# Uncut last weighted sums, both gate products behind the next filling product, and two low pieces moved to GpSimd

## The chip, the cores and the metric

The kernel runs on one core of a Trainium2 chip. The metric is the device time of one execution in microseconds (us); the median of several runs is compared. Five engines matter: TensorE (PE for matmuls, PEld for its weight loads), VectorE (DVE), ScalarE (ACT), GpSimd (POOL) and SyncE (SP, which here issues DMAs and reads expert numbers).

## What is computed

The reference is an attention in which a query sees only the keys of its own hash bucket, followed by a mixture of experts that gives each token to one expert.

```python
mask = q_bucket[:, :, :, None] == k_bucket[:, :, None, :]
scores = np.where(mask, scale * q @ k.T, -1e9)
attn = exp(scores - max) / (sum + 1e-9)
x = (attn @ v) as 3072 tokens x 512
logits = x @ w_gate;  e_idx = argmax(logits)
gate_w = softmax(logits)[e_idx];  eom = sigmoid(x @ w_output_gate)
out[token] = gate_w * eom[e_idx] * (relu(x @ w1[e]) @ w2[e])
```

There are 4 batches of 8 heads, 768 positions of 64 numbers; 8 experts with w1 of 512x1024 and w2 of 1024x512. Everything is float32.

## The kernel before, in words

**Products in three parts.** A float32 product of good precision is made of three products of rounded operands: each operand is split into a high part (rounded to the format fp32r) and a low part (operand minus high part), and high x high, high x low and low x high are summed (`product`, line 386). Making a low part is one subtraction with both inputs in the on-chip memory.

**Two phases.** Attention works through 16 pairs of heads in steps; at its end stands the switch to the experts. The 3072 tokens are routed batch by batch; the last batch's routing can only be finished when the last head pair is summed. To fill TensorE meanwhile, 256 tokens of the fullest expert, known from the first three batches, are gathered early, and the eight filling products `fill(0)` to `fill(7)` (w1 of that expert, 12 matmuls each, `up` line 386; ReLU on ScalarE, line 396; the low part on VectorE, line 397, called by `low()`) are laid between the steps of the last routing. All this is an order written out by hand: within that block each engine executes its instructions in the order of the program text, so an instruction that waits holds up those behind it on its engine.

**The place of the change** is this block. In order of the text it holds:

- `fill(0)`;
- the four pieces of the first w2, of 128x1024 numbers: the high parts (`w2_round`, lines 218 and 220) of pieces 2 and 3 on ScalarE, then the low parts (`w2_low`, line 225) of all four on VectorE. Before the third low part stand the three `late_low` subtractions (line 1124), halves of w1's low part, 128x512 each, on VectorE;
- the last weighted sums (`weighted`, line 764): six chunks of two matmuls each, accumulated in `ps_a`; after the sixth, VectorE copies the sum to the second half of the tile `ot` (line 767). After the first chunk's matmuls VectorE's transposition `rows` (line 787) of the first half of `ot` and its four DMAs on SP (line 794) stand in the order;
- `add_pair(hf, ...)`: three matmuls of 128 tokens each (line 831) that add the last head pair's share to the gate logits of half `hf` of the batch, and VectorE's addition (line 832). `add_pair(1)` reads the second half of `ot`;
- from there the routing's chain: `best`, `choose`, the transposition of the second half, `prefix`, `gates`, `ranks`, `cols`, `hot`, `table` (line 294), `entries`, with fills and lows between; then the second product of the early tokens (`down_rows`), the gathers, and the experts in order of their size.

The tiles of the four pieces rotate through five buffers named `w2l`: four hold the raw pieces, the first low part goes into the fifth, and the low part of piece i goes into the buffer of raw piece i-1.

Of the kernel before, what the change touches and what calls it, by code (L numbers as in the profile page):

```python
# [10 lines left out]
F32 = mybir.dt.float32  # L11
# [5 lines left out]
ALU = mybir.AluOpType  # L17
# [6 lines left out]
P = 128  # L24
# [35 lines left out]
def f32(ap):  # L60
    return ap.bitcast(F32)
# [3 lines left out]
def lsh_attention_then_moe(  # L65
# [10 lines left out]
    nc = tc.nc  # L76
# [17 lines left out]
    def signs():  # L94

        t = gp.tile([P, P], F32, name="t_ob")
        nc.scalar.dma_start(t, proj[:, D + 3:])
        return t
# [121 lines left out]
            e.tensor_scalar(hi, p[0], 1.0, 0.0, ALU.mult, ALU.add)  # L220
        return hi

    def w2_low(pool, p, hi):
        lo = pool.tile([P, 2, DM], F32R, name="w2l", bufs=NFB // 2 + 1)
        nc.vector.tensor_tensor(lo, p[0], f32(hi), ALU.subtract)
        return [(hi[:, j], lo[:, j]) for j in range(2)]

    def compared(e, out, x, y, op):
# [75 lines left out]
    ps_t = ctx.enter_context(tc.tile_pool(name="ps_t", bufs=2, space=PSUM))  # L304
    ps_a = ctx.enter_context(tc.tile_pool(name="ps_a", bufs=1, space=PSUM))
    ps_m = ctx.enter_context(tc.tile_pool(name="ps_m", bufs=1, space=PSUM))
# [204 lines left out]
    with ExitStack() as actx:  # L511
# [32 lines left out]
        def load(g, heads=(0, 1)):  # L544
            st = pairs[g]
            st.setdefault("qk", [])
            for j in heads:
                t = hp.tile([P, S], F32, name="qk", bufs=4)
                nc.sync.dma_start(t, qkT[2 * g + j])
                st["qk"].append(t)  # L550
# [15 lines left out]
        def project(g, pp=None, heads=(0, 1)):  # L566
            st = pairs[g]
            if pp is None:
                pp = ps_m.tile([P, HS], F32, name="ps_m")
            for j in heads:  # L570
                for m in range(2):
                    r = 32 * (2 * j + m)
                    nc.tensor.matmul(pp[r:r + 32], pjc[:, m], st["qk"][j][:, m * HS:(m + 1) * HS],
                                     start=True, stop=True)
            bt = hp.tile([P, HS], BF16, name="bt", bufs=2)
            rs = slice(D * heads[0], P)
            nc.vector.tensor_scalar(bt[rs], pp[rs], thr[rs], scl[rs], ALU.is_gt, ALU.mult)
            st["bt"] = bt
# [122 lines left out]
        def soft(s, sc, mn):  # L701
            if s % GROUP == 0:
                sums[s // GROUP] = terms[s // GROUP % len(terms)]
            pr = sc.rearrange("p a b -> p (a b)")
            k = s % GROUP
            nc.scalar.activation(pr, pr, AF.Exp, bias=mn, scale=-1.0,  # L706
                                 accum_out=sums[s // GROUP][:, k, 0:1])
            return pr

        def normal(s0):  # L710

            rs = sp.tile([P, GROUP], F32, name="rsum")
            nc.vector.tensor_reduce(rs, sums.pop(s0 // GROUP), AX.X, ALU.add)
            nc.vector.reciprocal(rs, rs)  # L714
            for k in range(GROUP):
                e = nc.vector if s0 + k == NSTEP - PER - GROUP else nc.gpsimd
                e.tensor_scalar(live[s0 + k], live[s0 + k], rs[:, k:k + 1], 0.0, ALU.mult, ALU.add)  # L717
# [79 lines left out]
        def routing(b):  # L797
# [26 lines left out]
                                        pm[:, :, 0:n, 0:2 * E].rearrange("p t i c -> p t c i"), AX.X, ALU.add)  # L824

            def add_pair(hf, i):
                pm = ps_m.tile([P, 3, 32], F32, name="ps_m")
                hs = slice(hf * 3, hf * 3 + 3)
                for t in range(3):
                    qs = slice((hf * 3 + t) * P, (hf * 3 + t + 1) * P)  # L830
                    nc.tensor.matmul(pm[:, t], pairs[b * H // 2 + i]["ot"][:, qs], wgt[:, i], start=True, stop=True)
                nc.vector.tensor_tensor(st["lgt"][:, hs], st["lgt"][:, hs], pm[:, :, 0:2 * E], ALU.add)
# [163 lines left out]
        for b in range(B - 1):  # L996
            r = routing(b)
# [12 lines left out]
        r = routing(B - 1)  # L1010
        s0 = 12 * (NP - 1)
        lp = H // 2 - 1
# [141 lines left out]
        with tc.manual_schedule(engines=MANUAL | {mybir.EngineType.SP}):  # L1154
            t = signs()
            load(0)
            load(1)
            for bb in halves[:2]:
                nc.vector.memset(bb, 0.0)
            for rs in terms:  # L1160
                nc.vector.memset(rs, 1e-9)
            make_identity(nc, ident)
            for bb in halves[2:]:
                nc.gpsimd.memset(bb, 0.0)

            idle = ps_t.tile([P, 3, P], F32, name="ps_t")

            def turn_idle(n):
                for i in range(n):
                    nc.tensor.transpose(idle[:, i % 3], ident, ident)  # L1170

            turn_idle(12)
            first_heads(t)
            turn_idle(1)
            live = {}
            raw = []

            def softs(n):
                for _ in range(n):
                    if raw:  # L1180
                        s = raw.pop(0)
                        live[s] = soft(s, *live[s])
                        if s % GROUP == GROUP - 1:
                            ready.append(s - s % GROUP)

            ready = []

            def normals():
                while ready:
                    normal(ready.pop(0))  # L1190

            def now(when):
                for fn in around.get((s, when), ()):
                    fn()

            for s in range(PER):
                live[s] = scores(s)
                raw.append(s)
                if 0 < s < PER - 1:
                    turn_idle(1)  # L1200
                if s > 2 and s % 2:
                    normals()
                softs(1)
                for fn in at.get(s, ()):
                    fn()

            for s in range(PER, NSTEP + LAG, 2):
                k = s % PER
                both = range(s, s + 2)
                for x in both:  # L1210
                    if x < NSTEP:
                        live[x] = scores(x)
                        raw.append(x)
                    if x == PER:
                        project(1)
                    if x == PER + 1:
                        for y in range(2):
                            transposed(y, live.pop(y))
                if k == 0 and s > PER:
                    softs(2)  # L1220
                    now("early")
                    normals()
                    now("amid")
                    softs(2)
                    normals()
                    for when in ("before", "matmuls", "behind"):
                        now(when)
                    softs(1)
                elif k == 4 or s == PER:
                    normals()  # L1230
                for x in both:
                    if s > PER:
                        transposed(x - LAG, live.pop(x - LAG))
                if s < 2 * PER or k == 0:
                    softs(1)
                for x in both:
                    for fn in at.get(x, ()):
                        fn()


            ep, hs = early["ep"], early["h"]
            w2s = []
            lows = []

            def fill(f):
                lows.append(up(early["w1"], early["x"], hs, [f], CAP0))

            def low():
                lows.pop(0)()

            fill(0)
            for i, (p, hi) in enumerate(zip(w2p, early["w2h"] + [w2_round(ep, p, nc.scalar) for p in w2p[2:]])):
                if i == 2:
                    for cc in range(1, NCC):
                        late_low(cc)
                w2s += w2_low(ep, p, hi)
            for c in range(NT):
                weighted(2 * NP - 1, c)
                if c == 0:
                    rows(NP - 1, 0, False)  # L1260
                if c == 2:
                    r["add_pair"](0, lp)
            fill(1)
            low()
            r["add_pair"](1, lp)
            fill(2)
            low()
            r["best"]()
            r["choose"]()
            rows(NP - 1, 1, False)  # L1270
            fill(3)
            low()
            r["prefix"]()
            fill(4)
            r["gates"]()
            low()
            r["ranks"]()
            fill(5)
            low()
            fill(6)  # L1280
            r["cols"]()
            low()
            fill(7)
            r["hot"]()
            r["table"]()
            low()
            r["entries"]()
            gid0 = lead_slots(EARLY)
            low()

    mp = ctx.enter_context(tc.tile_pool(name="mp", bufs=1, reuse_waits="tile"))
    with tc.manual_schedule(engines=MANUAL):
# [18 lines left out]
        for r in range(E):  # L1311
# [3 lines left out]
            if r:  # L1315
                hs = new_h()
                w2s = []
# [93 lines left out]
    with tc.If(nr > 0):  # L1411
# [12 lines left out]
        with tc.For_i(0, nr, 1):  # L1424
# [13 lines left out]
            for r in range(E):  # L1438
                more = nc.values_load(left[0:1, r:r + 1], min_val=0, max_val=NTOK)
                with tc.If(more > 0):  # L1440
                    w1s = [w1_piece(wpool, r, cc) for cc in range(NCC)]
                    w2s = []
# [64 lines left out]
```

## Time and profile before

| what | us |
|---|---|
| median of 3 runs (lowest to highest) | 686.34 (686.2 to 687.45) |
| the profiled execution | 686.96 |
| its span, first to last instruction | 685.1 |
| TensorE busy | 674.8 (98%) |
| VectorE, ScalarE, GpSimd busy | 472.6, 435.2, 407.9 |

The profiled execution took 1.86 us more than its span; that part lies outside all instructions. A time of a part is read in the trace as the distance between starts of instructions, since the durations of matmuls and of neighbours on one engine overlap a little.

### The profile page before, as it was taken

To read this page: it belongs to the slowest core of one execution; us is meant where nothing else is said; L and a number is where in the kernel's file an instruction comes from. 1 tells how busy PE (TensorE), PEld (TensorE's weight loads), DVE (VectorE), ACT (ScalarE), POOL (GpSimd) and SP (SyncE) were. 2 spreads that over 40 slices of the span, in tenths; PEclk is the share of its full clock that TensorE was granted. 3 is DMA by queue.
4 is the path that set the end of the run, shared out by engine and by line. 5 is a ranking of instruction groups with operands and counts; after the bars stand their busy time and mean duration, and the time that the engine had idled before them with its cause. 6 is when DMAs were issued, how large, how long until landed. Compare 5 with 4: busy or idle time off the path is not lost. (4 is left out here: it accounts for less than half of the span.)

```text
span 685.1 us, 17346 instructions
## 1 busy us (share of the span) xinstructions
PE 674.8 (98%) x6549; PEld 537.1 (78%) x6549; DVE 472.6 (69%) x1055; ACT 435.2 (64%) x889; POOL 407.9 (60%) x545
## 2 busy tenths in 40 slices
PE   8999999999999999999999999999999999999996
PEld 4767675767676767676767889889999999989995
DVE  7878887888877888878977834463646565646540
ACT  6898998898889898988998214431515243445041
POOL 6878766577856778656888156344273737374002
PEclk9999999999999999999999999999999999999998
DMA  5544554354543445442535135634667666665332
GB/s 167 162 125 101 132 123 109 78 131 104 130 118 82 111 114 118 107 112 59 144 101 175 24 106 193 207 107 149 222 193 235 210 207 220 216 222 198 124 98 79
DMA packets 96612, 96.14 MB, mean 140 GB/s; under 512 B 57839, under 2 KB 76839, under 8 KB 96520
## 3 DMA queue, kind: packets, MB, share of 16 engines
q1 hardware_dynamic: 79704, 72.88, 38.4%
q0 software_dynamic: 5200, 13.31, 5.7%
q10 hardware_dynamic: 11616, 8.75, 4.5%
q8 instruction: 54, 0.88, 0.6%
q14 instruction: 38, 0.31, 0.1%
HBM read 63.83 MB, written 17.50 MB: 119 GB/s over the span
## 5 line engine op out<-in xcount | busy, mean ns | idle before, releaser
L717 POOL TENSOR_SCALAR sc<-sc,rsum 128x768 f32<-128x768 f32 x191 | 171.5, 914 | 75.7 <-DVE rsum L714 35.4
L698 DVE TENSOR_SCALAR_CACHE_REDUCE sc<-ps_s 128x768 f32<-128x768 f32 x192 | 176.4, 955 | 22.1 <-PE ps_s L695 20.5
L706 ACT ACTIVATE sc<-sc,mn 128x768 f32<-128x768 f32 x192 | 178.9, 952 | 1.5 <-DVE sc L698 1.3
L695 PE MATMUL ps_s<-kh,qhl 64*128 64x384 f32 x768 | 149.1, 401 | 0.6 <-DMA qhl<-qhl 0.5
L764 PE MATMUL ps_a<-pts,vt 128*64 128x384 f32 x768 | 131.2, 490 | 0.0
L396 ACT ACTIVATE hh<-ps_s 128x256 fp32r<-128x256 f32 (+8 forms) x40 | 29.1, 727 | 157.8 <-PE ps_s L386 157.8
L753 ACT COPY pts<-ps_t 128x384 f32<-128x384 f32 x188 | 92.6, 494 | 24.2 <-PE ps_s L746 20.4
L764 PEld LDWEIGHTS ps_a<-pts,vt 128*64 128x64 f32 x768 | 52.3, 137 | 66.8 <-issue 61.5
L746 PEld LDWEIGHTS ps_t<-ident,sc 64*128 64x128 f32 x1140 | 81.9, 139 | 20.2 <-POOL sc L717 10.8
L386 PE MATMUL ps_s<-xh,w1h 128*128 128x256 f32 (+7 forms) x288 | 95.9, 333 | 0.0
L360 POOL DMA_INDIRECT xq<-x_dram,idx x75 | 82.0, 1093 | 23.2 <-issue 19.3
L386 PE MATMUL ps_s<-xlo,w1h 128*128 128x256 f32 (+7 forms) x288 | 95.6, 332 | 0.0
L386 PE MATMUL ps_s<-xh,w1l 128*128 128x256 f32 (+7 forms) x288 | 95.3, 331 | 0.0
L397 DVE SCALAR_TENSOR_TENSOR hl<-ps_s,hh 128x256 fp32r<-128x256 f32 (+8 forms) x40 | 34.0, 849 | 76.8 <-ACT hh L396 76.8
L746 PE MATMUL ps_t<-ident,sc 64*128 64x64 f32 x1140 | 86.8, 223 | 0.0
L695 PEld LDWEIGHTS ps_s<-kh,qhl 64*128 64x128 f32 x768 | 76.6, 187 | 1.7 <-DMA qhl<-qhl 0.8
L695 PE MATMUL ps_s<-kl,qhl 64*128 64x384 f32 x384 | 66.5, 333 | 0.0
L695 PE MATMUL ps_s<-bb 64*128 64x384 bf16 x384 | 65.3, 327 | 0.8 <-DMA bb<-bt 0.3
L372 POOL TENSOR_SCALAR xh<-xt 128x512 fp32r<-128x512 f32 (+5 forms) x21 | 12.0, 569 | 78.8 <-DVE xt L369 78.8
L386 PEld LDWEIGHTS ps_s<-xh,w1h 128*128 128x128 f32 x288 | 54.2, 188 | 1.8 <-issue 0.6
L753 ACT COPY pts<-ps_m 128x384 f32<-128x384 f32 x94 | 45.2, 481 | 15.6 <-PE ps_m L746 12.2
L386 PEld LDWEIGHTS ps_s<-xlo,w1h 128*128 128x128 f32 x288 | 54.1, 188 | 1.3 <-DVE xlo L343 0.2
(272 smaller groups left out, 1398.3 us busy)
## 6 DMA issues: line engine op xcount, KB each, us to landing
w_raw<-in_w_dram SPq DMA_DIRECT2D x31, 512.0 KB
qk<-in_qkT_dram SPq DMA_DIRECT2D x32, 384.0 KB
qhl<-qhl SPq DMA_DIRECT2D x62, 192.0 KB
xh<-in_w_dram SPq DMA_DIRECT2D x14, 512.0 KB
xlo<-in_w_dram SPq DMA_DIRECT2D x14, 512.0 KB
vt<-in_v_dram SPq DMA_DIRECT2D x16, 384.0 KB
x_dram<-xb SPq DMA_DIRECT2D x60, 96.0 KB
yt<-y_dram ACTq DMA_DIRECT2D x14, 256.0 KB
```

The costliest lines, as they stand in the source:

```text
L360: nc.gpsimd.indirect_dma_start(out=xq[:, k * P:(k + 1) * P], out_offset=None, in_=x_dram.rearrange("n (a f) -> (n a) f", a=NB32), in_offse ...
L372: nc.gpsimd.tensor_scalar(xh, w[:, :, 0:n], 1.0, 0.0, ALU.mult, ALU.add)
L386: nc.tensor.matmul(ps, l, r, start=first and k == 0, stop=last and k == len(pairs) - 1)
L396: nc.scalar.activation(hh, ph, AF.Relu)
L397: return lambda: nc.vector.scalar_tensor_tensor(hl, ph, 0.0, f32(hh), ALU.max, ALU.subtract)
L695: nc.tensor.matmul(ss[:, h, 0:HS], q[rs, c:c + P], k[rs, 0:HS], start=(i == 0), stop=(i == 3))
L698: nc.vector.tensor_scalar(sc, ss[:, :, 0:HS], MASKED, None, ALU.min, ALU.min, accum_out=mn)
L706: nc.scalar.activation(pr, pr, AF.Exp, bias=mn, scale=-1.0, accum_out=sums[s // GROUP][:, k, 0:1])
L717: e.tensor_scalar(live[s0 + k], live[s0 + k], rs[:, k:k + 1], 0.0, ALU.mult, ALU.add)
L746: nc.tensor.transpose(trs[h][:, c], pr[r, c * P:(c + 1) * P], ident[r, r])
L753: (nc.vector.tensor_copy if h and s and (last or s % PER == 0 or s in (3, 5)) else nc.scalar.copy)(pts[:, :, t * P + h * hq:t * P + (h + 1 ...
L764: nc.tensor.matmul(st["av"][n * D:(n + 1) * D], st["v"][:, n if g else hf, c], blocks[hb][n][:, c], start=(c == 0), stop=(c == NT - 1))
```

## The change

It does four things. The six chunks of the last weighted sums follow each other without `add_pair(0)` between the third and the fourth. Both `add_pair` calls stand behind `fill(1)`. `add_pair(0)` takes its accumulator from the two buffers `ps_t` instead of the single `ps_m`, for every caller. And the low parts of pieces 2 and 3 of the first w2 are made by GpSimd instead of VectorE; their place in the text, behind the `late_low` subtractions, stays.

```diff
-    def w2_low(pool, p, hi):
+    def w2_low(pool, p, hi, e):
         lo = pool.tile([P, 2, DM], F32R, name="w2l", bufs=NFB // 2 + 1)
-        nc.vector.tensor_tensor(lo, p[0], f32(hi), ALU.subtract)
+        e.tensor_tensor(lo, p[0], f32(hi), ALU.subtract)
         return [(hi[:, j], lo[:, j]) for j in range(2)]
...
             def add_pair(hf, i):
-                pm = ps_m.tile([P, 3, 32], F32, name="ps_m")
+                pool, name = (ps_m, "ps_m") if hf else (ps_t, "ps_t")
+                pm = pool.tile([P, 3, 32], F32, name=name)
...
                 if i == 2:
                     for cc in range(1, NCC):
                         late_low(cc)
-                w2s += w2_low(ep, p, hi)
+                w2s += w2_low(ep, p, hi, nc.vector if i < 2 else nc.gpsimd)
             for c in range(NT):
                 weighted(2 * NP - 1, c)
                 if c == 0:
                     rows(NP - 1, 0, False)
-                if c == 2:
-                    r["add_pair"](0, lp)
             fill(1)
             low()
-            r["add_pair"](1, lp)
+            for hf in range(2):
+                r["add_pair"](hf, lp)
             fill(2)
             low()
             r["best"]()
```

## Rows read from the trace of the kernel before

**Rows 1.** Busy time by stretch (us; PE, PEld, DVE, ACT, POOL; clock, DMA): the last full one

```profile
650.00:670.00 20.00, 20.00 (x111) 18.52 (x110) 8.29 (x8) 9.44 (x12) 1.99 (x2) 1.00 0.30 91
```

**Rows 2.** Timeline of TensorE (start, us, engine, line), switch to the experts

```profile
376.44 2.16 PE L764 MATMUL ps_a<-pts,vt 128*64 128x384 f32 x12
378.52 0.85 PE L831 MATMUL ps_m<-wgt,ot 128*128 128x32 f32 x6
379.31 2.16 PE L764 MATMUL ps_a<-pts,vt 128*64 128x384 f32 x12
381.39 0.39 PE L386 MATMUL ps_s<-xh,w1h 128*128 128x256 f32 x1
...
382.80 0.28 PE L386 MATMUL ps_s<-xh,w1l 128*128 128x256 f32 x1
383.53 0.86 PE L831 MATMUL ps_m<-wgt,ot 128*128 128x32 f32 x6 [0.45 <-DVE ot L767]
384.22 0.37 PE L386 MATMUL ps_s<-xh,w1h 128*128 128x256 f32 x1
```

**Rows 3.** Timeline of TensorE: the sums of an earlier half, uncut

```profile
356.04 4.09 PE L764 MATMUL ps_a<-pts,vt 128*64 128x384 f32 x24
360.06 0.27 PE L746 MATMUL ps_t<-ident,sc 64*128 64x64 f32 x1
```

**Rows 4.** Timeline of VectorE, same stretch

```profile
375.33 2.84 DVE L225 TENSOR_TENSOR w2l<-w2l,w2h 128x1024 fp32r<-128x1024 f32 x2
378.09 1.29 DVE L1124 TENSOR_TENSOR w1l<-w_raw,w1h 128x512 fp32r<-128x512 f32 x2
...
379.89 2.54 DVE L225 TENSOR_TENSOR w2l<-w2l,w2h 128x1024 fp32r<-128x1024 f32 x2
382.35 0.57 DVE L787 STREAM_TRANSPOSE xb<-ot 128x384 f32<-128x384 f32 x1
...
382.93 0.54 DVE L767 COPY ot<-ps_a 128x384 f32<-128x384 f32 x1
```

**Rows 5.** Timelines of ScalarE and GpSimd, same stretch

```profile
376.82 1.98 ACT L218 CAST w2h<-w2l 128x1024 fp32r<-128x1024 f32 x2
...
388.43 0.19 POOL L282 CAST t_gh<-gate 128x6 fp32r<-128x6 f32 x1 [12.64 <-DVE gate L882]
```

**Rows 6.** GpSimd's subtractions of two inputs: a group by shape, one pair in the timeline

```profile
L645 POOL TENSOR_TENSOR kl<-qk,kh 128x384 fp32r<-128x384 f32 x30 | 30.4, 1014 | 0.3
...
363.25 2.53 POOL L1119 TENSOR_TENSOR w1l<-w_raw,w1h 128x512 fp32r<-128x512 f32 x2
```

**Rows 7.** Timelines of VectorE and GpSimd: one two-input instruction, twice

```profile
11.64 0.56 DVE L642 SCALAR_TENSOR_TENSOR qhl<-qk,qhl 128x384 fp32r<-128x384 f32 x1
...
39.07 0.51 POOL L637 TENSOR_SCALAR kh<-qk 128x384 fp32r<-128x384 f32 x1
...
39.14 0.85 DVE L642 SCALAR_TENSOR_TENSOR qhl<-qk,qhl 128x384 fp32r<-128x384 f32 x1 [1.83 <-POOL qhl L636]
```

**Rows 8.** Timelines of GpSimd and VectorE: indirect DMAs beside subtractions

```profile
570.05 0.95 POOL L360 DMA_INDIRECT xq<-x_dram,idx  x1 [0.30 <-issue]
...
572.73 2.32 DVE L190 TENSOR_TENSOR w1l<-w_raw,w1h 128x1024 fp32r<-128x1024 f32 x2
...
572.86 1.88 POOL L360 DMA_INDIRECT xq<-x_dram,idx  x1 [0.30 <-issue]
```

**Rows 9.** Timelines: the end of the routing's chain, and w2's first use

```profile
391.52 1.23 POOL L274 TENSOR_TENSOR t_rhs<-t_rhs,t_gl 128x192 fp32r<-128x192 f32 x1
...
393.13 0.78 PE L294 MATMUL ps_t<-t_rhs,lt 128*128 128x128 f32 x6
393.75 0.45 PE L386 MATMUL ps_s<-w2h,hh 128*128 128x512 f32 x1
```

**Rows 10.** The last matmul (timeline of TensorE) and granted clock behind it (by stretch)

```profile
678.68 0.28 PE L386 MATMUL ps_a<-w2h,hl 128*96 128x256 f32 x1
...
681.00:682.00 1.00, 0.00 (x0) 0.00 (x0) 0.00 (x0) 0.00 (x0) 0.00 (x0) 0.62 0.61 174
```

## The prediction, made before the changed kernel was run

> **What bounds the kernel now.** I read the busy time by stretch first. TensorE is busy without a gap through the expert phase [rows 1], and the table of waits shows there nothing of TensorE that is worth naming. So whatever shifts the start of that dense stretch shifts the end by as much, and nothing later takes it back. The one place where the change can act is the switch to the experts, so the timelines of that stretch were next. TensorE runs there: half of the last sums, `add_pair(0)`, the other half, `fill(1)`, then a gap of 0.45 us before `add_pair(1)`, which waits for VectorE's copy to `ot`, then `fill(2)` at 384.22 [rows 2]. From there on it is dense again up to the table's matmuls at 393.13 [rows 9]. The reader is to see why the copy is late: the sums ended at about 381.3, but VectorE works from 375.33 without a pause through two low pieces, three late lows, two more low pieces and the transposition, and reaches the copy at 382.93 [rows 4]. GpSimd meanwhile idles 12.64 us, to 388.43 [rows 5]. My measure for everything below is the start of `fill(2)`: 384.22 before.
>
> **The sums and the products, part by part.** A half of the sums takes 2.08 us (376.44 to 378.52) and the two together 4.16; uncut, an earlier group of the same 24 matmuls takes 4.02, from 356.04 to 360.06 [rows 2, 3]. So the sums end at 376.44 + 4.02 = 380.46. `fill(1)` takes 1.53 (381.39 to the last of its twelve at 382.80, and that one's distance of 0.12 to a next), so it ends at 381.99. The first gate product costs 0.79 (378.52 to 379.31), the second 0.69 (383.53 to 384.22) [rows 2]. Side by side, and if nothing waits, they end at 381.99 + 0.79 + 0.69 = 383.47. That would be a gain of 384.22 - 383.47 = 0.75 us: 0.14 from the uncut sums and about 0.6 from the gap before the second product. A `ps_t` buffer for `add_pair(0)` I cost at nothing: the last transposition copies have left both long before, and the table's product takes the other of the two ten microseconds later.
>
> **What the second product waits for.** It needs the copy to `ot` by 381.99 + 0.79 = 382.78. If VectorE only lost two low pieces (2.54 us [rows 4]), its late lows would end at about 379.9, the transposition at 380.4, the copy, which then waits for the sums, at about 381.1. That is 1.7 us in hand. So the question is whether the pieces given to GpSimd leave VectorE alone.
>
> **GpSimd's price.** Its subtractions of two inputs take 1.014 us for 384 columns and 2.53 for two of 512, so 1.265 each [rows 6]. By the slope between the two a piece of 1024 costs 1.265 + 512 x 0.00196 = 2.27; by two of 512, 2.53. I take 2.4. The pieces themselves are not urgent: the second product of the early tokens starts at 393.75 [rows 9], and two pieces of 2.4 are done ten microseconds earlier even if they wait. When can they start? Their high parts come from ScalarE at 376.82 to 378.80 [rows 5]. The low part of piece 2 goes into the buffer of raw piece 1, which VectorE's second low piece reads until 378.17 (375.33 + 2.84). So GpSimd asks at about 378.2, just when VectorE has begun the first of its three late lows at 378.09 [rows 4].
>
> **Do they disturb each other?** Both kinds of instruction read two inputs from the on-chip memory. The same VectorE instruction takes 0.56 alone and 0.85 when GpSimd began 0.07 earlier an instruction of 0.51 (39.07 to 39.58): it went on at 39.14 + 0.85 - 0.56 = 39.43, 0.15 before GpSimd's end [rows 7]. Of the 29 executions of this line, 25 take 0.82 to 0.86, each begun inside such an instruction of GpSimd. So a VectorE instruction with two such inputs stands still while GpSimd's runs. Who gets in when both wait is shown in the expert phase: GpSimd's indirect DMA takes 0.95, and 1.88 when it begins at 572.86 inside the first of two back-to-back subtractions; the delay of 0.93 ends at 573.79, at the boundary of the two, not behind the second, which ends at 575.05 [rows 8]. Four more indirect DMAs that fall into such pairs do the same. So the one that waits gets in at the next boundary.
>
> **The sum.** A late low takes 0.60 from start to start ((379.89 - 378.09) / 3 [rows 4]). The first ends at 378.69. GpSimd, waiting since 378.2, gets in and runs to 381.09; VectorE goes on 0.15 before that, at 380.94, and ends its second late low at 381.54. GpSimd's second piece, waiting by then, runs to 383.94. The third late low goes on at 383.79 and ends at 384.39. The transposition takes 0.49 (382.35 to its successor at 382.84), the copy 0.54, TensorE starts 0.06 behind it (383.47 to 383.53 before): 384.39 + 0.49 + 0.54 + 0.06 = 385.48. The second product takes 0.69, and `fill(2)` starts at 386.17, 1.95 us later than before. What is queued behind the copy on VectorE (the low part of `fill(0)`, both additions to the logits, all of the routing's chain) moves along; so do TensorE's `fill(2)` and everything behind it, and SP's eight DMAs of the two halves of rows, which follow their transpositions. Nothing in that stretch has spare time to take it back: the last input of the table is ready at 392.75 (391.52 + 1.23) for matmuls at 393.13 [rows 9]. Against the profiled execution, 686.96 + 1.95 = 688.9; against the median of 686.34, **688.3**. The bounds: 2.27 a piece gives 1.95 - 0.26 = 1.7; 2.53 a piece and no early release (0.15 twice) gives 1.95 + 0.26 + 0.3 = 2.5. So 688.0 to 688.9 for this case.
>
> The Trainium skill ("SBUF — State Buffer", section "Who interferes with whom") says that a VectorE instruction with two on-chip inputs and a GpSimd instruction that reads there exclude each other, the first holding the shared ports for its whole length. The trace agrees but for the 0.15 us. By the page alone, with 2.4 a piece, the sum would be 2.25 and the time 688.6.
>
> **The rivals.**
> - *VectorE keeps its place (chance 0.26).* Each piece of GpSimd's that gets in between late lows costs the copy about 2.25 us; with 1.7 in hand, the first costs little and the second decides. If GpSimd's second piece doesn't get in before the third late low, the copy ends near 383.17 and `fill(2)` starts at 383.92: 0.3 gained, 686.0. If neither gets in, all 0.75 is gained, 685.6; then both pieces run behind the late lows, to about 384.7, beside the transposition and the copy, which read one on-chip input or none. For it: no row shows a GpSimd subtraction of 1024 columns, nor one waiting through back-to-back subtractions (the indirect DMA's read is short). Against it: rows 7 and 8 together. This case ends on the other side: not slower.
> - *The clock falls in the new gap (0.10).* TensorE would wait from 382.78 to 385.48, 2.7 us. At the end of the program the last matmul ends at 678.96 and the mean granted clock of the microsecond from 681.00 is 0.62, so it fell from 1.0 to the half level (1.2 GHz) at about 681.24, 2.3 us behind it [rows 10]. No wait of before is that long within the work, and no row shows how long the half level would last. Below, nothing; above, all from `fill(2)` to the table (8.9 us of work [rows 2, 9]) at half speed, 8.9 more. I take one fill, 1.5 us: 689.8. Against it: work surrounds this gap, and only idle follows the other.
> - *The gain is larger than the gap and the cut (0.04).* All that I can add is what the second product's addition gains on VectorE, 0.1; for over 0.2% a stretch would have to be shortened that the trace shows dense.
> - *It does not move (0.06)*: a hold and a half of GpSimd's, or a smaller piece, which eats up the 0.75 and stops there; 686.3.
>
> **How the numbers follow.** 0.2% of this kernel, 1.4 us, is about what a measurement can tell from no change. The forecast (chance 0.54) and the fallen clock (0.10) lie above it: slower 0.64. The cases of 0 to -0.75 us, 0.26 + 0.06, lie within: same 0.32. Faster 0.04. The time is the likeliest case's, 688.3, with its own 688.0 to 688.9. The range goes below to the full gain, 685.4 with the runs' scatter (686.2 to 687.45 before), and above to 690.0, which takes in the short fall of the clock; the long one, and the larger gain, stay out.
>
> **What would show it.** Right: GpSimd's two `w2_low` pieces of 2.3 to 2.6 us in the timeline at about 378.3 and 381.1, the second and third late lows stretched to over 2 us each, the copy to `ot` ending at about 385.4, a gap of 2.5 to 3 us on TensorE before `add_pair(1)`, and `fill(2)` near 386.2 with everything behind it shifted alike. Uncut sums of 4.0 us show the first part; an `add_pair(0)` that waits for the copy too would add 0.8. Wrong: late lows of 0.68 in a row with GpSimd's first piece behind them, a copy done by 382.7 and no gap; or a granted clock below 1.00 between 385 and 390.

## The result, and the profile after

The changed kernel takes a median of 690.26 us (689.39 to 692.76, 7 runs) against 687.40 us for the kernel before (686.20 to 688.33, 7 runs). The ratio is 1.0051, with a 95% interval of 1.0041 to 1.0060: slower by about half a per cent. The forecast was 688.3 in a range of 685.4 to 690.0, so the direction was right and the time lies just above the range. The profiled execution took 690.1 us, with a span of 688.4 us, 3.3 us more than the span before.

The timeline of TensorE in the switch to the experts, in the kernel after (start, us, engine, line; code behind `w2_low` stands one line lower than before), answers to [rows 2]:

```profile
374.37 0.47 PE L821 MATMUL ps_m<-ident,lt 96*128 96x96 f32 x3
...
376.21 4.09 PE L764 MATMUL ps_a<-pts,vt 128*64 128x384 f32 x24
380.23 0.39 PE L386 MATMUL ps_s<-xh,w1h 128*128 128x256 f32 x1
...
381.77 0.75 PE L832 MATMUL ps_t<-wgt,ot 128*128 128x32 f32 x6
385.05 1.23 PE L832 MATMUL ps_m<-wgt,ot 128*128 128x32 f32 x6 [2.53 <-DVE ot L767]
386.08 0.56 PE L386 MATMUL ps_s<-xh,w1h 128*128 128x256 f32 x1
...
388.79 0.28 PE L386 MATMUL ps_s<-xh,w1h 128*128 128x256 f32 x1
...
396.19 0.78 PE L294 MATMUL ps_t<-t_rhs,lt 128*128 128x128 f32 x6
```

The sums run uncut, the two products stand behind `fill(1)`, and the second waits 2.53 us for the copy to `ot`, where it waited 0.45 before. The reason stands in the timeline of VectorE (after; answers to [rows 4]) and in that of GpSimd (after; answers to [rows 5]):

```profile
375.10 2.83 DVE L225 TENSOR_TENSOR w2l<-w2l,w2h 128x1024 fp32r<-128x1024 f32 x2
377.84 3.46 DVE L1125 TENSOR_TENSOR w1l<-w_raw,w1h 128x512 fp32r<-128x512 f32 x2
381.22 2.85 DVE L1125 TENSOR_TENSOR w1l<-w_more,w1h 128x512 fp32r<-128x512 f32 x1
383.99 0.56 DVE L787 STREAM_TRANSPOSE xb<-ot 128x384 f32<-128x384 f32 x1
384.48 0.51 DVE L767 COPY ot<-ps_a 128x384 f32<-128x384 f32 x1
```

```profile
378.15 5.37 POOL L225 TENSOR_TENSOR w2l<-w2l,w2h 128x1024 fp32r<-128x1024 f32 x2 [2.61 <-ACT w2h L218]
```

GpSimd begins its first piece at 378.15, inside the first late low. Two of the three late lows then take over 2 us longer than they do alone: the first two together 3.38 from start to start (377.84 to 381.22) instead of 1.20, the third 2.77 (381.22 to 383.99) instead of 0.60. Of the columns of the next view, busy time by stretch of the kernel after (PE, PEld, DVE, ACT, POOL, then granted clock of TensorE, DMA share, GB/s), the clock is the one to read:

```profile
382.00:384.00 2.00, 0.52 (x5) 0.41 (x4) 2.00 (x2) 0.35 (x1) 1.51 (x1) 1.00 0.00 0
384.00:386.00 2.00, 0.95 (x6) 0.95 (x6) 1.44 (x5) 0.00 (x0) 0.00 (x0) 0.84 0.17 29
386.00:388.00 2.00, 2.00 (x11) 2.00 (x11) 1.52 (x8) 0.00 (x0) 0.00 (x0) 0.50 0.40 69
388.00:390.00 2.00, 2.00 (x16) 2.00 (x16) 1.41 (x6) 0.65 (x3) 0.00 (x0) 0.81 0.13 22
```

From 386 to 388 TensorE is busy without a pause and does 11 matmuls, where the fills at full clock, with a matmul every 0.12 us, have some 17: the granted clock is 0.50, the lower level (1.2 GHz). `fill(2)` therefore takes 2.71 us (386.08 to 388.79) instead of 1.50 (384.22 to 385.72 before).

**Where the 3.3 us are.** I measure from the last transposition on TensorE that stands before the block (line 821; 374.60 before, 374.37 after). The timeline of TensorE before, the lines that stand in no row above:

```profile
374.60 0.47 PE L821 MATMUL ps_m<-ident,lt 96*128 96x96 f32 x3
...
385.72 0.28 PE L386 MATMUL ps_s<-xh,w1h 128*128 128x256 f32 x1
```

| distance from line 821, us | before | after | difference |
|---|---|---|---|
| second gate product starts | 8.93 | 10.68 | +1.75 |
| `fill(2)` starts | 9.62 | 11.71 | +2.09 |
| the table's matmuls start (line 294) | 18.53 | 21.82 | +3.29 |

The late copy costs 1.75. The clock costs 3.29 - 1.75 = 1.54: 0.34 in the second product (1.03 instead of 0.69) and 1.20 from `fill(2)` to the table (10.11 instead of 8.91). From the table to the end of the span it is 292.0 before and 292.2 after, so nothing is taken back later, and no more than 0.2 is added.

### The profile page after: what moved, and what is told of

Same layout as the page of the kernel before. It is cut to its first block, busy times and chain, and to the rows that moved or that the text cites. A ratio compares the mean times of both kernels' runs of the same rounds, so it can differ in the third digit from the quotient of the medians.

```text
span 688.4 us, 17350 instructions
## 1 busy us (share of the span) xinstructions
PE 676.4 (98%) x6549; PEld 538.7 (78%) x6549; DVE 474.8 (69%) x1053; ACT 435.0 (63%) x889; POOL 411.8 (60%) x547
## 5 line engine op out<-in xcount | busy, mean ns | idle before, releaser
L386 PEld LDWEIGHTS ps_s<-xh,w1l 128*128 128x128 f32 x288 | 54.8, 190 | 1.1
```

Source lines behind the costliest of these rows:

```text
L386: nc.tensor.matmul(ps, l, r, start=first and k == 0, stop=last and k == len(pairs) - 1)
```

## The experiments

The theory after the result: GpSimd's two pieces, each begun between two late lows, hold VectorE for their whole length; that makes the copy late; and TensorE's standstill of 2.5 us lets its clock fall. The rivals: the new order of sums and products costs the time; or the clock falls for another reason than the standstill (GpSimd's or the DMAs' activity).

The runs were made on other chips, on which the kernel before takes 691 to 698 us. There TensorE also waits in the expert phase, for example 1.10 us for VectorE's low part at 590.80 in a run of the kernel before, and single times of the kernel before on one chip range from 693.57 to 700.97 us. So the stage from line 821 to the table is the measure here, and the ratios of whole times stand beside it. A run of the unchanged kernel on one of those chips gave the stage again as 18.53, and from the table to the end of the span 296.9 instead of 292.0. So that chip's extra time lies mostly behind the stage, and I take the stage as comparable from chip to chip. All columns but the ratio come from one profiled execution each; before_again, pool_again, half_warm and vector_gap were executed only once.

| run | ratio to before (95%) | stage, us | to `fill(2)` | `fill(2)` to table | wait of the second product | clock in the stage |
|---|---|---|---|---|---|---|
| before | | 18.53 | 9.62 | 8.91 | 0.45 | 1.00 |
| before_again | | 18.53 | 9.62 | 8.91 | 0.44 | 1.00 |
| after | 1.0051 (1.0041 to 1.0060) | 21.82 | 11.71 | 10.11 | 2.53 | half level for 3.4 |
| after_again | 1.0041 (1.0023 to 1.0058) | 23.26 | 11.99 | 11.27 | 2.54 | half level for 6.8 |
| order_only | 1.0002 (0.9983 to 1.0021) | 18.46 | 9.51 | 8.95 | 0.67 | 1.00 |
| pool_only | 1.0007 (0.9987 to 1.0027) | 20.42 | 11.50 | 8.92 | 2.33 | 1.00 |
| pool_again | | 23.35 | 12.12 | 11.23 | 2.33 | half level for 6.8 |
| keep_warm | 1.0008 (0.9989 to 1.0028) | 20.29 | 11.39 | 8.90 | 0.77 | 1.00 |
| half_warm | | 20.28 | 11.37 | 8.91 | 1.63 | 1.00 |
| vector_gap | | 22.86 | 12.41 | 10.45 | 3.58 | half level for 3.4 |
| halves | 0.9996 (0.9975 to 1.0017) | 18.13 | 9.22 | 8.91 | 0.38 | 1.00 |
| late_first | 0.9971 (0.9952 to 0.9990) | 18.37 | 8.65 | 9.72 | none | 1.00 |
| one_piece | 0.9978 (0.9958 to 0.9999) | 17.56 | 8.66 | 8.90 | none | 1.00 |
| old_one_piece | 0.9947 (0.9929 to 0.9965) | 17.81 | 8.91 | 8.90 | none | 1.00 |

**order_only and pool_only: each half of the change by itself.** The first is the changed kernel with all four low pieces on VectorE, the second the kernel before with the two pieces on GpSimd.

```diff
 order_only, against the changed kernel
-                w2s += w2_low(ep, p, hi, nc.vector if i < 2 else nc.gpsimd)
+                w2s += w2_low(ep, p, hi, nc.vector)
 pool_only, against the kernel before (and w2_low with its argument e)
-                w2s += w2_low(ep, p, hi)
+                w2s += w2_low(ep, p, hi, nc.vector if i < 2 else nc.gpsimd)
```

> The new order of sums and gate products, all four low pieces on VectorE. Port theory (the loss comes from GpSimd's pieces standing between VectorE's late lows): VectorE reaches the copy at about 382.9 as before, the second gate product waits some 0.6 us, the granted clock stays 1.00, and the time is 0 to 0.4 us below before. Order theory (both products behind the filling product cost the time): most of the loss of the change stays, 2 to 3.5 us above before.

> The old order, with GpSimd making low pieces 2 and 3. Port theory: the late lows stretch to over 2 us as in the changed kernel, the copy is done near 385.4, TensorE stands still over 2 us in front of the second gate product, and the time is 2 to 3.5 us above before. Order theory: VectorE is relieved of 2.5 us, the copy comes earlier, and the time is 0.5 us below before.

The order alone changes the stage by -0.07 us. The pieces alone delay `fill(2)` by 1.88 us. The timelines of VectorE and GpSimd in pool_only show the same picture as after the whole change:

```profile
377.44 3.44 DVE L1124 TENSOR_TENSOR w1l<-w_raw,w1h 128x512 fp32r<-128x512 f32 x2
380.80 2.86 DVE L1124 TENSOR_TENSOR w1l<-w_more,w1h 128x512 fp32r<-128x512 f32 x1
...
377.74 5.38 POOL L225 TENSOR_TENSOR w2l<-w2l,w2h 128x1024 fp32r<-128x1024 f32 x2 [2.61 <-ACT w2h L218]
```

So the loss belongs to the pieces, and the rival of the order falls. The whole time of pool_only rose by 0.07% where its stage of 1.89 us more would make 0.27%, the upper edge of its interval, and more in executions like pool_again, below; whether waits of the expert phase on that chip hide the rest was not settled. Its profiled execution is the fastest of its twelve (693.30; the median is 697.01), so its clock of 1.00 need not be the rule.

**halves: the same work of GpSimd in shorter instructions.** If VectorE stands for one whole instruction of GpSimd at each boundary, instructions of half the length must halve each hold.

```diff
-        e.tensor_tensor(lo, p[0], f32(hi), ALU.subtract)
+        for j in range(2) if e is nc.gpsimd else (slice(0, 2),):
+            e.tensor_tensor(lo[:, j], p[0][:, j], f32(hi)[:, j], ALU.subtract)
```

> The changed kernel with each of GpSimd's two subtractions cut into two of 512 columns: the same work in GpSimd, in four instructions of about 1.3 us. If VectorE waits for one whole instruction of GpSimd at each boundary: the second and third late low take about 1.8 us each instead of 2.8, the copy ends 2.2 to 2.6 us earlier than in the changed kernel, the second gate product waits under 0.8 us, the clock stays 1.00, and from the last token transposition to the table it is 0 to 0.5 us less than before (18.53 us). If VectorE waits for all of GpSimd's queued work, or the two share the port evenly: the copy as late as in the changed kernel and the stage 1.7 to 3.3 us longer than before.

The timelines of VectorE and GpSimd (one line lower again):

```profile
378.75 2.36 DVE L1126 TENSOR_TENSOR w1l<-w_raw,w1h 128x512 fp32r<-128x512 f32 x2
381.04 1.77 DVE L1126 TENSOR_TENSOR w1l<-w_more,w1h 128x512 fp32r<-128x512 f32 x1
...
379.06 6.11 POOL L226 TENSOR_TENSOR w2l<-w2l,w2h 128x512 fp32r<-128x512 f32 x4 [2.61 <-ACT w2h L218]
```

The first two late lows take 2.29 from start to start instead of 3.38 and the third 1.77 instead of 2.85, each 1.1 less. The number of holds stays, and the length of each follows GpSimd's instruction. The copy comes in time to leave a wait of 0.38, and the stage gains 0.40 on before although GpSimd still does both pieces.

**one_piece and old_one_piece: no piece between the late lows.** GpSimd makes only the low part of piece 3, in the new order and in the old one.

```diff
-                w2s += w2_low(ep, p, hi, nc.vector if i < 2 else nc.gpsimd)
+                w2s += w2_low(ep, p, hi, nc.vector if i < 3 else nc.gpsimd)
```

> The changed kernel with only piece 3 on GpSimd. Its low part goes into the buffer that VectorE's third low piece reads, so GpSimd can begin only behind all late lows. Port theory: late lows 0.6 to 0.7 us each, the copy on time, no gap of TensorE in front of the second gate product, and from the last token transposition to the table 0.6 to 0.8 us less than before (18.53 us). If what costs is GpSimd's work as such, in proportion: half of the change's loss, 0.9 to 1.7 us more than before.

> The order of before, with only piece 3 on GpSimd. Port theory: no late low is stretched, the copy is done before fill(1) ends, no gap, and from the last token transposition to the table 0.5 to 0.7 us less than before (18.53 us): the freed VectorE is worth about 0.6 us and the new order of sums and products (17.56 with one piece) only the rest, 0.1 to 0.4. If the new order is what brings the gain: within 0.2 us of before.

That low part goes into the buffer of raw piece 2, which VectorE's third low part reads behind the late lows. So the buffers themselves keep GpSimd out until then. The timelines of VectorE, GpSimd and TensorE in one_piece:

```profile
377.24 1.28 DVE L1125 TENSOR_TENSOR w1l<-w_raw,w1h 128x512 fp32r<-128x512 f32 x2
378.45 0.68 DVE L1125 TENSOR_TENSOR w1l<-w_more,w1h 128x512 fp32r<-128x512 f32 x1
379.05 1.22 DVE L225 TENSOR_TENSOR w2l<-w2l,w2h 128x1024 fp32r<-128x1024 f32 x1
...
380.68 0.52 DVE L767 COPY ot<-ps_a 128x384 f32<-128x384 f32 x1
...
380.49 2.36 POOL L225 TENSOR_TENSOR w2l<-w2l,w2h 128x1024 fp32r<-128x1024 f32 x1 [5.55 <-PE ps_a L764]
...
381.74 0.83 PE L832 MATMUL ps_m<-wgt,ot 128*128 128x32 f32 x6
382.41 0.37 PE L386 MATMUL ps_s<-xh,w1h 128*128 128x256 f32 x1
```

GpSimd starts 0.22 behind the end of that third low part (379.05 + 1.22 = 380.27); the releaser on its line, the sums, is the trace's inference and had ended before. The late lows run at 0.6 each, GpSimd's 2.36 us lie beside the copy, which has one input and keeps its 0.52, and the second product waits for nothing. The stage is 0.97 us shorter than before, the best of all, and the whole time 0.22% (0.01 to 0.42%). In the old order the stage is 0.72 shorter. So the piece taken off VectorE is worth 0.72, and the order, once the copy is in time, 0.25. By whole time old_one_piece is at -0.53%, more than the 0.10% that its stage explains; no trace of the kernel before stands here from that chip, so where the rest lies stays open. Both are below the kernel before, one_piece only just clear of the noise.

**late_first: the late lows ahead of everything GpSimd touches.**

```diff
-                if i == 2:
+                if i == 0:
                     for cc in range(1, NCC):
                         late_low(cc)
```

> The changed kernel with the three late lows ahead of the first w2 low piece instead of behind the second: the same work on the same engines, but no VectorE instruction with two on-chip inputs stands beside GpSimd's pieces until the routing. Port theory: late lows of 0.6 to 0.7 us, no gap of TensorE over 0.3 us, fill(2) 0.5 to 0.8 us earlier than before, time 0.5 to 0.8 us below before. If GpSimd's pieces slow VectorE whatever it does, or come too late for the second product of the early tokens: 1 us or more above before.

The copy is in time and `fill(2)` starts 0.97 us earlier than before, but the stage gains only 0.16; I had expected 0.5 to 0.8. GpSimd's pieces now stand beside the routing's chain. The timelines of GpSimd, VectorE and TensorE:

```profile
380.79 4.85 POOL L225 TENSOR_TENSOR w2l<-w2l,w2h 128x1024 fp32r<-128x1024 f32 x2 [4.46 <-DVE w2l L225]
...
381.13 0.56 DVE L767 COPY ot<-ps_a 128x384 f32<-128x384 f32 x1 [0.17 <-PE ps_a L764]
...
384.69 1.02 DVE L840 TENSOR_TENSOR df<-lgt,mx 128x48 f32<-128x48 f32 x1
...
387.72 0.39 PE L386 MATMUL ps_s<-xh,w1h 128*128 128x256 f32 x1 [0.44 <-DVE hl L397]
```

A subtraction of 48 columns in `best` takes 1.02 us instead of 0.21: it too has two inputs on chip and stands until GpSimd ends at 385.64. The chain behind it is late, and part of what the copy gave is lost there. The hold is moved, not removed. The whole time fell by 0.29%, about 2 us, which this stage doesn't explain; like that of old_one_piece it stays open.

**keep_warm and half_warm: the standstill filled.** 16 (or 8) transpositions of the identity into a `ps_t` buffer stand between the two gate products; their result is used by nobody.

```diff
+            warm = ps_t.tile([P, 3, P], F32, name="ps_t")
             for hf in range(2):
                 r["add_pair"](hf, lp)
+                if hf == 0:
+                    for i in range(16):
+                        nc.tensor.transpose(warm[:, i % 3], ident, ident)
```

> The changed kernel with 16 transpositions of the identity (about 2.4 us, results unused) between the two gate products, where TensorE stands still. Clock theory (the fall of the granted clock behind the gap costs about 1.3 us beyond the late copy): granted clock 1.00 from 384 to 390, fill(2) takes 1.5 us, time 1.0 to 1.5 us below the changed kernel, some 2 us above before. If the copy alone costs the time, or the transpositions delay the second product: same as the changed kernel or above.

> The changed kernel with 8 instead of 16 transpositions in the gap (about 1.2 us of it filled). Clock theory: the rest of the gap, 1.4 to 1.9 us, is shorter than what the clock survived with the old order (2.3 us), so clock 1.00 and a stage of 20.3 us. If the clock counts all idle time of the stretch, it falls and the stage takes over 21.3 us.

The copy stays as late as after the change (`fill(2)` 1.77 and 1.75 behind before), but the clock stays at 1.00 and `fill(2)` to table takes 8.90 and 8.91. The stages are 1.76 and 1.75 above before: without the fall only the late copy is left. Busy time by stretch of half_warm, which still leaves a recorded wait of 1.63 us:

```profile
384.00:386.00 2.00, 0.54 (x5) 0.30 (x3) 2.00 (x3) 0.00 (x0) 0.64 (x1) 1.00 0.00 0
386.00:388.00 2.00, 1.83 (x15) 1.83 (x16) 1.43 (x8) 0.00 (x0) 0.00 (x0) 1.00 0.43 74
```

GpSimd's work and the late copy are the same as after the change, and the clock didn't fall. That speaks for the standstill as the cause. It is not only these two executions: the mean granted clock of a whole execution averages 0.996 over keep_warm's twelve, as over the 35 of the kernel before on that chip, while the changed kernel's ten in after_again average 0.992 (0.990 to 0.994), against 0.996 for 27 of the kernel before beside them. By whole time keep_warm is 0.08% above before (-0.11 to +0.28%), where I had expected some 2 us, about 0.3%.

**vector_gap: a standstill without GpSimd.** order_only, with four more subtractions of 512 columns on VectorE ahead of the transposition. They write over half of the last of the four low pieces, so the result lacks the low part of an eighth of w2.

```diff
                 w2s += w2_low(ep, p, hi, nc.vector)
+            for _ in range(2):
+                nc.vector.tensor_tensor(w2s[-1][1], f32(w2s[-1][0]), f32(w2s[-2][0]), ALU.subtract)
+                nc.vector.tensor_tensor(w2s[-1][1], f32(w2s[-1][0]), f32(w2s[-2][0]), ALU.subtract)
```

> The new order with all four low pieces on VectorE, and four more subtractions of 512 columns on VectorE in front of the transposition (they overwrite the low part of the last eighth of w2 with another difference, so this part of the sum is wrong): the copy is late by VectorE's own work, 2.4 us, and GpSimd stands still. If the clock falls because TensorE stands still: a gap of 2.7 to 3.2 us in front of the second gate product, the granted clock falls to the half level behind it, and the stage from the last token transposition to the table takes 22 to 24 us. If the fall needs GpSimd and VectorE working side by side: clock 1.00 and 20.9 us.

The second product waits 3.58 us with GpSimd idle, and the clock falls as well. Busy time by stretch:

```profile
384.00:386.00 2.00, 0.27 (x3) 0.27 (x3) 1.97 (x6) 0.00 (x0) 0.00 (x0) 1.00 0.00 0
386.00:388.00 2.00, 2.00 (x13) 2.00 (x13) 1.37 (x8) 0.00 (x0) 0.00 (x0) 0.61 0.58 98
388.00:390.00 2.00, 2.00 (x12) 2.00 (x11) 1.31 (x5) 0.65 (x3) 0.00 (x0) 0.53 0.00 0
```

GpSimd's column is 0.00 from 376 to 390, so the rival that GpSimd's activity at that time pulls the clock down falls. That of the DMAs falls with half_warm: the same DMAs, and no fall.

**after_again, pool_again and before_again: how firm is it?** The changed kernel, pool_only and the kernel before, once more on other chips.

> The changed kernel once more. If the fall of the clock belongs to the gap of 2.5 us: the granted clock falls again behind it and the stage from the last token transposition to the table takes 21.8 us; if it came by the moment only: clock 1.00 and about 20.3 us, as with the old order and GpSimd's pieces (20.42).

> The old order with GpSimd's two pieces once more. If a gap of 2.3 us is too short for the clock to fall: clock 1.00 and a stage of 20.4 us again. If the first look was luck: half level behind the gap and 21.5 to 23.5 us.

> The kernel before, unchanged, on a chip of the experiments, where all kernels take some 9 us more than in the first runs. If the extra time lies behind the switch to the experts: the stage from the last token transposition to the table again 18.5 us with clock 1.00, and from the table to the end of the span 297 to 302 us instead of 292. If the switch itself is slower there: the stage 20 us or more.

after_again is slower by 0.41% (0.23 to 0.58%), and its clock falls for longer: its stage is 4.73 over before, 1.44 more than the first time. pool_again is the same program as pool_only with the same recorded wait of 2.33 us, and here the clock fell. Busy time by stretch, first pool_only, then pool_again:

```profile
384.00:386.00 2.00, 1.24 (x10) 1.24 (x11) 1.39 (x6) 0.00 (x0) 0.00 (x0) 1.00 0.29 49
386.00:388.00 2.00, 2.00 (x19) 2.00 (x18) 1.79 (x9) 0.65 (x3) 0.00 (x0) 1.00 0.29 49
```

```profile
384.00:386.00 2.00, 1.14 (x6) 1.15 (x6) 1.13 (x4) 0.00 (x0) 0.00 (x0) 0.64 0.29 49
386.00:388.00 2.00, 2.00 (x10) 2.00 (x10) 1.45 (x7) 0.00 (x0) 0.00 (x0) 0.50 0.29 49
388.00:390.00 2.00, 2.00 (x11) 2.00 (x11) 1.36 (x6) 0.65 (x3) 0.00 (x0) 0.50 0.10 18
390.00:392.00 2.00, 2.00 (x18) 1.92 (x18) 0.97 (x8) 0.38 (x1) 0.39 (x2) 0.65 0.47 80
```

With the clock up the stage is 20.42, with the clock down 23.35: the fall costs 2.93 us there. So a wait of this length can go either way, and what it costs ranges from nothing to about 3 us (after_again: 4.73 in the stage less 1.76 for its late copy). What decides between the two executions no view here shows.

The traces of the experiments hold more such cases, behind the stage: on those chips TensorE also waits in the expert phase, and there too the clock fell, for example in order_only (timeline of TensorE, then busy time by stretch), with GpSimd idle:

```profile
593.90 0.44 PE L386 MATMUL ps_s<-xh,w1h 128*128 128x384 f32 x1 [1.85 <-DVE hl L397]
```

```profile
594.00:596.00 2.00, 2.00 (x9) 2.00 (x10) 2.00 (x2) 2.00 (x3) 0.00 (x0) 0.74 0.92 238
596.00:598.00 2.00, 2.00 (x7) 2.00 (x7) 2.00 (x3) 1.32 (x2) 0.00 (x0) 0.50 0.95 243
```

In the fourteen traces of this case the clock falls twelve times before the last matmul, each time behind a recorded wait of TensorE of 1.83 us or more. Of the eighteen such waits twelve were followed by a fall: five of the ten of 1.83 to 1.94 us, and seven of the eight of 2.33 to 3.58. So the fall goes with the standstill and not with this place of the kernel, and a gap shorter than the one here can bring it.

## Why the prediction was out of its range

**Right: the new order gives little by itself.** The uncut sums took 4.02 (376.21 to 380.23), as forecast from [rows 3]. Of the 0.75 us that the order and the freed VectorE could give together, order_only shows 0.07 for the order while the copy is late, and one_piece 0.97 for both when the copy is early. My ceiling of 0.75 was too low by what two neighbouring products save: in one_piece they take 1.26 together (381.15 to 382.41), where I had added up 0.79 and 0.69 from separate places.

**Right: the two engines take turns at instruction boundaries.** From [rows 7, 8] I expected GpSimd to get in behind the first late low and again behind the second, each piece holding VectorE for its length less 0.15. Both holds are there. I had put 2.25 for each; they measure 2.18 (3.38 - 1.20) and 2.17 (2.77 - 0.60), and the second product starts 1.75 later, where I had 1.95, within my 1.7 to 2.5. order_only against pool_only shows that it comes from the pieces, halves that the length of GpSimd's instruction sets it. The Trainium skill ("SBUF — State Buffer", section "Who interferes with whom") says that such a pair excludes each other for the whole instruction, and the trace agrees but for the ends: a hold of 2.17 belongs to a piece that takes 2.36 in one_piece, where nothing holds it.

**Right: nothing takes it back.** The table to the end of the span is 292.0 before and 292.2 after.

**Wrong: the chance of the rival "the clock falls in the new gap".** The step that failed is the sentence "Against it: work surrounds this gap, and only idle follows the other", with the chance of 0.10 that I drew from it. The recorded gap was 2.53 us, as I had forecast (2.7), and [rows 10] had shown a fall within 2.3 us of the last matmul. Work on either side of the gap did not protect it: of four executions in which the second product waited 2.33 to 2.54 us the clock fell in three, and in vector_gap's 3.58 it fell too, while in this stage it stayed at 1.00 in the eight experiments whose gap was filled, shorter or absent. In the expert phase of the experiments it fell behind waits from 1.83 us on, in the middle of dense work. A rival that my own forecast of the gap made likely got a tenth of the chance. Its price was nearly right for the profiled execution: I took one fill at half speed, 1.5 us and 689.8; it cost 1.54, and 686.34 + 3.29 gives 689.6. That it fits so well is luck: in pool_again and after_again the fall cost 2.9 and 3.0.

**Wrong with it: the top of the range.** I set 690.0 just above that price and left the long fall out. Had the fall been the likeliest case, its own bounds (nothing to 8.9 us more) would have taken the top well past it; after_again and pool_again show falls of 6.8 us each. The sum also started too low: the median of before over 7 runs is 687.40, 1.06 above the median of the 3 that it started from. Either error alone would have left the time within the range: 686.34 + 3.29 is 689.63, and 687.40 + 1.75, the late copy without the fall, is 689.15. Together they give 690.7, and 690.26 was measured. The chances of the three outcomes had slower in front, at 0.64, and half a per cent slower is what came.

## What to carry to other kernels

Before moving two-input work to an idle GpSimd, see what VectorE does in the same microseconds: if it is a row of two-input subtractions on the path, GpSimd comes in at each boundary and VectorE pays the longer instruction, so place the piece behind that row (one_piece, -0.97 us) or cut it short (halves, -0.40) rather than count only the work that VectorE loses. When a change opens a gap like those seen here (1.8 to 3.6 us) in a TensorE that is the bound, price the work behind it at the lower clock as a likely case and not as a remote one; 8 transpositions with unused results in the gap kept the clock here. And measure a stage from a fixed instruction before it to one after it when the whole time scatters by more than the effect.

## What was not expected of the hardware

- The clock fell in one execution and stayed in another with the same program and the same recorded wait of 2.33 us (pool_again, pool_only). Once down, it stayed at the half level for 3.4 us in ten of the twelve falls and for 6.8 in two, under unbroken work; in the switch to the experts a fall cost 1.5 to 3.0 us. In the expert phase it fell behind five of ten waits of 1.83 to 1.94 us.
- Even a VectorE instruction of 48 columns, 0.21 us alone, is held by a GpSimd subtraction of two inputs (1.02 us in late_first), so the small instructions of a chain can be held as well as the large ones.
- GpSimd's subtraction of 1024 columns takes 2.36 us where no VectorE instruction with two inputs in the on-chip memory stands beside it (one_piece); the estimate from [rows 6] was 2.4.
